# Window attention and a gated MLP on one core: the hidden units dealt to partitions in groups of four

## The chip, the cores and the metric

The kernel runs on 1 core of one Trainium2 chip. The metric is device time in microseconds (us) of one execution. Before the change the median of 3 runs is 228.85 us (227.75 to 229.1).

## The reference

Sliding-window attention with four sink positions, then an MLP whose activation has a learned slope for each hidden unit. Inputs and output are float32; the kernel computes in bf16 with float32 sums.

```python
B, H, S, D = 4, 8, 768, 64            # n_sink = 4, window = 128
scores = scale * np.matmul(q, k.transpose(0, 1, 3, 2))
keep = is_sink | in_window            # pos < 4, or 0 <= i - j < 128
scores = np.where(keep, scores, -1000000000.0)
a = softmax(scores)
x = np.matmul(a, v)                   # as (3072 tokens, 512)
...
h = x @ w_in                          # w_in (512, 2048)
g = h * (1.0 / (1.0 + np.exp(-beta * h)))   # beta (2048,)
out = g @ w_out                       # w_out (2048, 512)
```

## The kernel before

**Tiles and stages.** The 3072 tokens are cut into 8 tiles of 384. An attention *unit* n (of 32) is one pair of heads for one tile: q and k are transposed so that the 64 head elements lie on partitions, scores are taken 128 keys at a time, ACT takes the exponential, DVE multiplies by the mask, PE multiplies with v, DVE normalises. Four units fill `xT` for one tile (512 model elements on 4 x 128 partitions).

The MLP of a tile has 16 *blocks* m of 128 hidden units (`NM` = 16). For one block PE runs four matmuls (c = 0 to 3) of 384 columns into one PSUM bank: the stationary operand is a 128 x 128 piece of `w_in16`, the moving one a piece of `xT` (L814, "hidden matmul"). ACT takes tanh of beta/2 times the result (L822; the scale is a column of `beta_half`, one value for each partition), and DVE makes `g` (L835). The projection (L843) then multiplies `g[:, m, 128 tokens]` (stationary) with `w_out16[:, m, :]` (moving, 512 columns) and sums over the 16 blocks. Which hidden unit lies on which partition of which block is free, as long as w_in's columns, beta and w_out's rows agree.

**Layouts in memory.** Before, block m holds the units 128m to 128m+127, unit 128m+p on partition p. w_in is loaded in 4 pieces of 512 columns by POOL (L578), w_out in 8 pieces of two blocks by POOL (L583), both cast to bf16 by the DMA. In a w_out piece each partition gets two rows of w_out that lie 128 rows apart in memory. beta comes as a 16 x 128 tile by one DMA on ACT's queue (L864), is transposed by PE with a float32 identity (L883) and halved by DVE (L885).

**Order of the work.** Operations are declared in program order, with what they read and write. A planner (`Prog`) then places them: for each engine it takes the operation that can start first, with durations written into the code and an estimate of when each DMA lands. What comes out is one fixed order per engine, with semaphore waits in it. Changed transfers therefore change the order on all engines, and each engine works strictly in that order.

**Queues.** SP issues the float32 loads of q and k for units 0 to 11 (L522). POOL casts them to bf16 (L621; at the start DVE casts q), and issues the loads of w_in, w_out, v (L542), and, for units 12 and up, the landing DMAs of q, k (L552) and v (L561), which SP then turns with DMA transposes (L567). POOL does its casts and its DMA issues in one order.

Some loads are gated on others by `after`, so that they do not crowd the DMA engines: unit n of 8 to 11 waits for the w_out piece that holds block 2n-12, and two v loads wait for the pieces of blocks 6 and 8 (L969 to L978). The units 4 to 7 wait for w_in's second piece.

Of the kernel before, what the change touches and what calls it, by code (L numbers as in the profile page):

```python
# [5 lines left out]
F32 = mybir.dt.float32  # L6
AF = mybir.ActivationFunctionType
ALU = mybir.AluOpType

B, H, S, D = 4, 8, 768, 64  # L10
NSINK, WINDOW = 4, 128
DM, DF, NOUT = 512, 2048, 512
NTOK = B * S
NPAIR = B * (H // 2)
SCALE = 1.0 / (D ** 0.5)
# [3 lines left out]
TT = 384  # L19
NT = NTOK // TT  # L20
NU = 4 * NT
NM = DF // 128
# [33 lines left out]
AGENDA = {}  # L56
for n in range(4, 8):
    for step, at in (("in", n - 4), ("sink", 16), ("a", 16), ("b", 16), ("av", 17), ("out", 18)):
        AGENDA.setdefault(at if step == "in" else at + 1 * (n - 4), []).append((n, step))
for n in range(8, NU):  # L60
    for at, step in STEPS.items():
        AGENDA.setdefault(FIRST[n] + at, []).append((n, step))
# [294 lines left out]
def bass_streamingllm_window__then__act_swish_beta_kernel(  # L357
# [21 lines left out]
    def sb(name, shape, dtype):  # L379
        ctx.append(nc.sbuf_tensor(name, list(shape), dtype))  # L380
        return ctx[-1].__enter__()
# [5 lines left out]
    xT = sb("xT", (128, 4, NTOK), BF16)  # L387
    w_in16 = sb("w_in16", (128, 4, DF), BF16)
    w_out16 = sb("w_out16", (128, NM, NOUT), BF16)
    beta_stage = sb("beta_stage", (16, 128), F32)  # L390
    beta_half = sb("beta_half", (128, NM), F32)
    ones = sb("ones", (128, 128), BF16)
    zeros = sb("zeros", (128, 384), BF16)
    ident = sb("ident", (128, 128), BF16)
    ones32 = sb("ones32", (32, 32), F32)
    ident32 = sb("ident32", (32, 32), F32)
    scratch = sb("scratch", (32, 1), F32)
    mask = [sb(f"mask{z}", (128, 6, 128), BF16) for z in range(2)]
    add_mask = sb("add_mask", (128, 6, 128), BF16)
# [25 lines left out]
    op = P.op  # L425

    def pe(n):
        return {"busy": 2.5 + n / 2.4, "lag": 260.0}
# [4 lines left out]
    def dve(t):  # L433
        return {"busy": t, "lag": 140.0}
# [4 lines left out]
    def select(out_ap, in_ap, patt, cmp, fill, base, cm, r, w, after=()):  # L439
        op("gp", lambda e: e.affine_select(out_ap, in_ap, patt, cmp, fill, base=base,  # L440
                                           channel_multiplier=cm), r=r, w=w, busy=290.0, lag=100.0, after=after)
# [75 lines left out]
    def load_qk(n, x, after=(), queue="sp"):  # L517
        _, _, half, pb = place(n)
        name = "qk"[x]
        s = rows_of((q, k)[x], n, 1, half, 3)  # L520
        d = stage[name][pb][:, :, 3 * half:3 * half + 3, :].rearrange("p h c d -> p h (c d)")
        op(queue, lambda e: e.dma_start(d, s), w=[(name + "_stage", pb, half)], after=after,  # L522
           dma=f"{name}{pb}_{half}", seq="loads " + queue, **transfer(2 * TT * D * 4, 290 if n not in (1, 2) or x else 170, 520.0))

    def load_v32(x, c):

        src = v[0, 4 * x:4 * x + 4, c * 128:c * 128 + 128, :].rearrange("h p d -> p h d")
        op("act", lambda e: e.dma_start(v_stage[:, c, 4 * x:4 * x + 4, :], src), w=[("v_stage", x, c)],
           dma=f"v{x}{c}", seq="loads act", **transfer(4 * 128 * D * 4, 240, 520.0, 0.45))
# [41 lines left out]
           w=[("qkT", pb, half)], dma=f"t{pb}{half}", busy=1300.0, lag=1300.0)  # L571

    w_in_src = moe_w_in.rearrange("(c p) f -> p c f", p=128)
    w_out_src = moe_w_out.rearrange("(m p) n -> p m n", p=128)

    def load_w_in(m, ms, after=()):
        here = slice(m * 128, (m + ms) * 128)
# [2 lines left out]
           dma=f"wi{m}", late=0.0 if m else 800.0, **transfer(DM * ms * 128 * 4, 385, 740.0, 3.0))  # L580

    def load_w_out(m, ms, after=()):
        op("gp", lambda e: e.dma_start(w_out16[:, m:m + ms, :], w_out_src[:, m:m + ms, :]), after=after,  # L583
           w=[("w_out", mm) for mm in range(m, m + ms)],
           dma=f"wo{m}", **transfer(ms * 128 * NOUT * 4, 416, 740.0, 3.0))

# [224 lines left out]
    def hidden_matmul(i, c):  # L811
        T, m = i // NM, i % NM
        bank, name = hidden_bank(i)
        op("pe", lambda e: e.matmul(  # L814
            bank, w_in16[:, c, m * 128:(m + 1) * 128], xT[:, c, T * TT:(T + 1) * TT],
            start=(c == 0), stop=(c == 3)),
           r=[("w_in", c, m), ("xT", T, c)], w=[name], **pe(TT))

# [22 lines left out]
    def project(T, t, m, bank, name, eng="act", cols=slice(0, NOUT), queue="sp"):  # L841
# [19 lines left out]


    constants()
    op("act", lambda e: e.dma_start(beta_stage[:, :], moe_beta.rearrange("(m p) -> m p", p=128)),  # L864
       w=["beta_stage"], dma="beta", busy=500.0, lag=100.0)
    for n in range(4):
        for x in range(2):
            load_qk(n, x)
    for c in range(6):
        load_v32(c // 3, c % 3)  # L870
    op("act", lambda e: e.activation(scratch[:, :], ones32[:, 0:1], AF.Exp, bias=0.0, scale=1.0),
       r=["ones32"], w=["scratch"], busy=1500.0)
    cast(0)
# [4 lines left out]
    cast(2)  # L878
    load_sinks(1, [("v", 1, 0, 0)])

    select(ident32[:, :], ones32[:, :], [[1, 32]], ALU.is_equal, 0.0, 0, -1, ["ones32"], ["ident32"])
    transpose_first(0)
    op("pe", lambda e: nc.tensor.transpose(acc[1][:, 0:16], beta_stage[:, :], ident32[0:16, 0:16]),  # L883
       r=["beta_stage", "ident32"], w=["acc1"], **pe(64))
    op("dve", lambda e: e.tensor_scalar(beta_half[:, :], acc[1][:, 0:16], 0.5, None, ALU.mult),  # L885
       x=["acc1"], w=["beta"], **dve(100.0))

    def first_scores(n):
        pairs = [("s0", "s1"), ("h0", "h1")] if n < 3 else [("s0", "s1"), ("tr", "av")]
# [48 lines left out]
    for s in range(-2, S_END + NM):  # L938
# [27 lines left out]
        if s in casts:  # L966
            cast(casts[s])
        if s == 0:
            for m in range(2, 8, 2):  # L969
                load_w_out(m, 2, [("w_in", 0, 0)])  # L970
        if s == 2:
            for m in range(8, NM, 2):
                load_w_out(m, 2, [("w_in", 0, 8)])
            for n in range(8, 12):
                for x in range(2):
                    load_qk(n, x, [("w_out", 2 * n - 12)])
            for c in range(2):
                load_v(2, c, [("w_out", 2 * c + 6)])  # L978
        if s == 23:
            load_v(2, 2)  # L980
        if s in lands:
# [59 lines left out]
```

## Time and profile before

| what | value |
|---|---|
| median of 3 runs | 228.85 us (227.75 to 229.1) |
| the profiled execution | 228.59 us, its span 226.9 us |
| granted TensorE clock | 1.0 throughout |
| PE busy | 220.0 us (97% of the span), 1761 matmuls |
| ACT, DVE, POOL busy | 141.3, 132.6, 125.7 us |
| DMA packets | 96901, 28.92 MB |

The span is what lies between the first and the last instruction; 1.7 us of the execution are outside it. The costliest groups and the transfers that matter here:

```profile
L822 ACT ACTIVATE th<-h_ps,beta_half 128x384 f32<-128x384 f32 x120 | 69.4, 581 | 59.7 <-PE h_ps L814 59.1
L843 PE MATMUL acc<-w_out,g 128*128 128x512 bf16 x368 | 99.7, 380 | 0.0
L814 PE MATMUL h_ps<-xT,w_in 128*128 128x384 bf16 x480 | 96.2, 326 | 0.0
...
q_stage<-in_q_dram SPq DMA_DIRECT2D x12, 192.0 KB, 7.4
k_stage<-in_k_dram SPq DMA_DIRECT2D x12, 192.0 KB, 7.9
w_in<-in_moe_w_in_dram POOLq DMA_DIRECT2D x4, 512.0 KB, 6.8
w_out<-in_moe_w_out_dram POOLq DMA_DIRECT2D x8, 256.0 KB, 9.6
```

A group's line gives the source line, the engine, what it writes and reads, its shape and count, then its busy us, the mean ns of one, and the idle time before it with its releaser. The mean of a matmul (326 ns) is longer than the distance between two, since matmuls overlap in the array. A DMA line gives the KB that one issue writes and the median us from issue to landing. "PEld" is the load of stationary weights, "SPq" and "POOLq" are issues by these engines' queues.

### The profile page before, as it was taken

The page shows a single profiled execution, that of the slowest core. Times are in us where ns is not written, and L with a number is a line of the kernel's source. Part 1 is how long each engine was busy: PE and PEld are TensorE (multiplying, and loading weights), DVE is VectorE, ACT ScalarE, POOL GpSimd, SP SyncE. Part 2 cuts the span into 40 slices and gives each one's busy share as a digit, 9 for nine tenths or more (in the row PEclk, how much of TensorE's full clock was granted, in tenths as well). Part 3 has the DMA queues.
Part 4 walks back from the last instruction along what each step waited for, and adds up shares of the span by engine and source line. Part 5 has one row for each costly group of instructions (what it writes and reads, how often), then busy time and mean ns, then how long its engine had stood idle before and what let it go on. Part 6 is the DMA issues. An engine that isn't in the chain of part 4 may idle for free.

```text
span 226.9 us, 4463 instructions
## 1 busy us (share of the span) xinstructions
PE 220.0 (97%) x1761; PEld 122.1 (54%) x1761; DVE 132.6 (58%) x264; ACT 141.3 (62%) x224; POOL 125.7 (55%) x191
## 2 busy tenths in 40 slices
PE   7999989999999999999999999999999999999995
PEld 4665545555555555555555555555555555555454
DVE  5466777488975776566565656555656564443200
ACT  1877796197586877566657766666656755555311
POOL 4689992899994979695939396876300000000000
PEclk9999999999999999999999999999999999999999
DMA  6999999999998999999999999998921012110122
GB/s 172 251 172 179 276 194 205 257 228 139 118 138 124 124 117 151 120 167 144 116 113 135 99 138 147 96 165 119 94 80 53 20 57 64 49 46 0 58 83 92
DMA packets 96901, 28.92 MB, mean 127 GB/s; under 512 B 83424, under 2 KB 93936, under 8 KB 96880
## 3 DMA queue, kind: packets, MB, share of 16 engines
q0 software_dynamic: 59232, 10.92, 65.7%
q1 hardware_dynamic: 34304, 16.79, 34.3%
q10 hardware_dynamic: 3344, 0.93, 1.9%
q8 instruction: 14, 0.23, 0.5%
q14 instruction: 7, 0.06, 0.1%
HBM read 27.34 MB, written 6.29 MB: 148 GB/s over the span
## 4 chain that ended last, share of the span: by engine, by line
PE 73%; DMA 15%; POOL 8%; issue 2%; SPq 1%; ACT 0%; POOLq 0%; ACTq 0%
PE acc L843 32%; PE h_ps L814 29%; DMA k_stage<-in_k_dram 8%; DMA w_out<-in_moe_w_out_dram 4%; PE s_ps L727 4%; PE s_ps L770 4%; POOL qk L621 3%; DMA w_in<-in_moe_w_in_dram 2%; POOL land L552 2%; PE h_ps L843 2%; POOL v_aug L561 1%; PE s_ps L759 1%; PE s_ps L670 1%; SPq L522 1%; POOL v_aug L532 0%
## 5 line engine op out<-in xcount | busy, mean ns | idle before, releaser
L822 ACT ACTIVATE th<-h_ps,beta_half 128x384 f32<-128x384 f32 x120 | 69.4, 581 | 59.7 <-PE h_ps L814 59.1
L843 PE MATMUL acc<-w_out,g 128*128 128x512 bf16 x368 | 99.7, 380 | 0.0
L814 PE MATMUL h_ps<-xT,w_in 128*128 128x384 bf16 x480 | 96.2, 326 | 0.0
L835 DVE SCALAR_TENSOR_TENSOR g<-th,h_ps 128x384 bf16<-128x384 f32 x120 | 65.6, 550 | 44.8 <-ACT th L822 44.0
L814 PEld LDWEIGHTS h_ps<-xT,w_in 128*128 128x128 bf16 x480 | 45.6, 98 | 39.8 <-issue 0.8
L843 PEld LDWEIGHTS acc<-w_out,g 128*128 128x128 bf16 x368 | 32.8, 98 | 28.8 <-issue 3.6
L552 POOL DMA_DIRECT2D land<-in_q_dram x40 | 30.2, 760 | 24.0 <-DVE rden L779 24.0
L552 POOL DMA_DIRECT2D land<-in_k_dram x40 | 30.3, 761 | 0.0
L561 POOL DMA_DIRECT2D v_aug<-in_v_dram x40 | 30.2, 760 | 0.0
L735 ACT ACTIVATE E<-s_ps 128x1536 bf16<-128x1536 f32 x20 | 28.8, 1442 | 0.0
L741 DVE TENSOR_TENSOR E<-E,mask 128x1536 bf16<-128x1536 bf16 x20 | 19.2, 958 | 16.4 <-ACT E L735 16.4
L851 ACT ACTIVATE out_sb<-acc 128x512 f32<-128x512 f32 x23 | 13.7, 596 | 7.6 <-PE acc L843 7.4
L770 PEld LDWEIGHTS s_ps<-v_aug,E 128*128 128x128 bf16 x336 | 15.2, 97 | 3.2 <-issue 1.2
L770 PE MATMUL s_ps<-v_aug,E 128*128 128x65 bf16 x336 | 16.8, 193 | 0.0
L707 ACT ACTIVATE E<-s_ps 128x768 bf16<-128x768 f32 x17 | 13.7, 811 | 4.3 <-PE s_ps L700 4.2
L781 DVE TENSOR_TENSOR o_norm<-s_ps,rden 128x384 bf16<-128x384 f32 x28 | 15.6, 556 | 0.8
L714 DVE TENSOR_TENSOR E<-E,mask 128x768 bf16<-128x768 bf16 x16 | 9.0, 572 | 2.0 <-ACT E L707 1.3
L727 PE MATMUL s_ps<-qkT 64*128 64x256 bf16 (+2 forms) x144 | 10.1, 254 | 0.0
L759 PE MATMUL s_ps<-v_sink,E_sink 128*128 128x130 bf16 x48 | 9.3, 219 | 0.0
L621 POOL CAST qk<-k_stage 128x384 bf16<-128x384 f32 x12 | 6.5, 544 | 4.7 <-DMA k_stage<-in_k_dram 4.4
L673 ACT ACTIVATE E_sink<-s_ps 128x384 bf16<-128x384 f32 x16 | 7.8, 490 | 1.5 <-PE s_ps L670 1.5
L727 PEld LDWEIGHTS s_ps<-qkT 64*128 64x128 bf16 x144 | 4.9, 94 | 7.1 <-issue 5.8
(75 smaller groups left out, 155.2 us busy)
## 6 DMA issues: line engine op xcount, KB each, us to landing
out_dram<-out_sb SPq DMA_DIRECT2D x23, 256.0 KB, 2.7
q_stage<-in_q_dram SPq DMA_DIRECT2D x12, 192.0 KB, 7.4
k_stage<-in_k_dram SPq DMA_DIRECT2D x12, 192.0 KB, 7.9
w_in<-in_moe_w_in_dram POOLq DMA_DIRECT2D x4, 512.0 KB, 6.8
w_out<-in_moe_w_out_dram POOLq DMA_DIRECT2D x8, 256.0 KB, 9.6
land<-in_q_dram POOLq DMA_DIRECT2D x40, 48.0 KB, 3.7
land<-in_k_dram POOLq DMA_DIRECT2D x40, 48.0 KB, 4.0
v_aug<-in_v_dram POOLq DMA_DIRECT2D x40, 48.0 KB, 3.4
```

What stands on the lines that cost most here:

```text
L552: op("gp", lambda e, d=d, s=s: e.dma_start(d, s), w=[("land", pb, half, x, hh)], after=after, dma=f"l{pb}{half}{x}{hh}", **transfer(TT * D ...
L561: op("gp", lambda e, d=d, s=s: e.dma_start(d, s), w=[("v", pb, 3 * half + c, hh) for c in range(3)], after=after, dma=f"lv{pb}{half}{hh}", ...
L707: op("act", lambda e: e.activation(both, src[:, :, 0:TT], AF.Exp, bias=0.0, scale=SCALE), x=list(names), w=[("E", n % NE, c)], **act(768))
L727: op("pe", lambda e, at=at, w=w, kb=kb, qb=qb, nq=nq, hh=hh, rows=rows, bank=bank: e.matmul(s_ps[:, 2 * hh + bank, at:at + w], keys_of(pb, ...
L735: op("act", lambda e: e.activation(E[z][:, :, :], src, AF.Exp, bias=0.0, scale=SCALE), x=list(S_NAMES), w=[("E", z, 0), ("E", z, 1)], **ac ...
L741: op("dve", lambda e: e.tensor_tensor(E[z][:, :, :], E[z][:, :, :], m.unsqueeze(1).to_broadcast([128, 2, 768]), ALU.mult), r=[("E", z, 0), ...
L770: last=(x == len(kbs) - 1): e.matmul(av_ps[:, at + hh * D1:at + hh * D1 + D1], E[z][:, hh, col:col + 128], v_aug[:, pb, hh, kb, 0:D1], sta ...
L781: op("dve", lambda e: e.tensor_tensor(o_norm[o][:, :, :, :].rearrange("p m h d -> p (m h) d"), src[:, :, 0:D], rden[z][:, :].unsqueeze(2). ...
L814: op("pe", lambda e: e.matmul(bank, w_in16[:, c, m * 128:(m + 1) * 128], xT[:, c, T * TT:(T + 1) * TT], start=(c == 0), stop=(c == 3)), r= ...
L822: op("act", lambda e: e.activation(th[i % 3][:, :], bank, AF.Tanh, bias=0.0, scale=beta_half[:, m:m + 1]), x=[name], r=["beta"], w=[("th", ...
L835: op("dve", lambda e: e.scalar_tensor_tensor(g[T % 2][:, m, :], th[i % 3][:, :], 1.0, bank, ALU.add, ALU.mult), r=[("th", i % 3)], x=[name ...
L843: op("pe", lambda e: e.matmul(bank[:, 0:width], g[T % 2][:, m, t * 128:(t + 1) * 128], w_out16[:, m, cols], start=(m == 0), stop=(m == NM ...
```

## The change

Hidden unit 512g + 4p + j now lies on partition p of block 4g + j (`PER` = 4). So on one partition the four rows of w_out of a group g are neighbours in memory, 8 KB in a row. Three layouts follow.

- w_out is loaded in 5 pieces of 2, 2, 4, 4, 4 blocks; in each piece a partition reads one run of 4 or 8 KB instead of two runs of 2 KB.
- w_in is loaded as before. The stationary operand of a hidden matmul is now every fourth column of a group of 512.
- beta is read by DMA straight into (128, 16): 4 runs of 16 bytes on each partition. The DMA is issued on ACT's queue behind the six first loads of v instead of ahead of them. The float32 identity, the PE transpose and PSUM bank use for it are gone; DVE halves beta from SBUF.

The gates of units 8 to 11 move to the pieces of blocks 0, 4, 8 and 12, those of the two v loads to blocks 8 and 12.

```diff
+PER = 4
...
-    beta_stage = sb("beta_stage", (16, 128), F32)
+    beta_raw = sb("beta_raw", (128, NM), F32)
...
-    ident32 = sb("ident32", (32, 32), F32)
...
-    w_out_src = moe_w_out.rearrange("(m p) n -> p m n", p=128)
+    w_out_src = moe_w_out.rearrange("(g p j) n -> p g j n", p=128, j=PER)
...
     def load_w_out(m, ms, after=()):
-        op("gp", lambda e: e.dma_start(w_out16[:, m:m + ms, :], w_out_src[:, m:m + ms, :]), after=after,
+        op("gp", lambda e: e.dma_start(w_out16[:, m:m + ms, :].rearrange("p j n -> p (j n)"),
+                                         w_out_src[:, m // PER, m % PER:m % PER + ms, :].rearrange("p j n -> p (j n)")), after=after,
...
-            bank, w_in16[:, c, m * 128:(m + 1) * 128], xT[:, c, T * TT:(T + 1) * TT],
+            bank, w_in16[:, c, m // PER * 512 + m % PER:m // PER * 512 + 512:PER], xT[:, c, T * TT:(T + 1) * TT],
...
-    op("act", lambda e: e.dma_start(beta_stage[:, :], moe_beta.rearrange("(m p) -> m p", p=128)),
-       w=["beta_stage"], dma="beta", busy=500.0, lag=100.0)
...
+    op("act", lambda e: e.dma_start(beta_raw[:, :].rearrange("p (g j) -> p g j", j=PER),
+                                   moe_beta.rearrange("(g p j) -> p g j", p=128, j=PER)),
+       w=["beta_raw"], dma="beta", busy=500.0, lag=300.0)
+    op("dve", lambda e: e.tensor_scalar(beta_half[:, :], beta_raw[:, :], 0.5, None, ALU.mult),
+       r=["beta_raw"], w=["beta"], **dve(100.0))
...
-    select(ident32[:, :], ones32[:, :], [[1, 32]], ALU.is_equal, 0.0, 0, -1, ["ones32"], ["ident32"])
...
-    op("pe", lambda e: nc.tensor.transpose(acc[1][:, 0:16], beta_stage[:, :], ident32[0:16, 0:16]),
-       r=["beta_stage", "ident32"], w=["acc1"], **pe(64))
-    op("dve", lambda e: e.tensor_scalar(beta_half[:, :], acc[1][:, 0:16], 0.5, None, ALU.mult),
-       x=["acc1"], w=["beta"], **dve(100.0))
...
         if s == 0:
-            for m in range(2, 8, 2):
-                load_w_out(m, 2, [("w_in", 0, 0)])
+            load_w_out(2, 2, [("w_in", 0, 0)])
+            load_w_out(4, 4, [("w_in", 0, 0)])
         if s == 2:
-            for m in range(8, NM, 2):
-                load_w_out(m, 2, [("w_in", 0, 8)])
+            for m in range(8, NM, 4):
+                load_w_out(m, 4, [("w_in", 0, 8)])
             for n in range(8, 12):
                 for x in range(2):
-                    load_qk(n, x, [("w_out", 2 * n - 12)])
+                    load_qk(n, x, [("w_out", 4 * (n - 8))])
             for c in range(2):
-                load_v(2, c, [("w_out", 2 * c + 6)])
+                load_v(2, c, [("w_out", 4 * c + 8)])
```

The planner's new order differs from the old one mostly where the transfers do. On POOL: the stretch from the first w_out issue to the casts of units 8 to 11 reads as follows (casts are "unit, operand"; `land` is a landing DMA of L552, `v` a load of L542, `lv` one of L561).

```
before: w_out 0, 4q, 4k, w_out 2, 5q, w_out 4, 5k, w_out 6, 6q, 6k, w_out 8, 7q, 7k, w_out 10, 12, 14,
        v, land q, v, land q, land k, land k, 8q, 8k, v, 9q, 9k, land q x2, 10q, 10k, land k x2, lv x2, ..., 11q, ..., 11k
after:  w_out 0, 4q, 4k, w_out 2, 5q, 5k, w_out 4, 6q, w_out 8, 6k, 7q, w_out 12, 7k,
        8q, land q x2, land k, v, land k, 8k, v x2, 9q, 9k, land q x2, land k x2, lv, 10q, 10k, lv, 11q, 11k
```

On PE, the two score matmuls of unit 7 that stood ahead of the first projections now stand behind the first eight of them, and the transposes of units 8 to 10 are split into a group for q and one for k with other work between them; the rest moves by a few matmuls. On DVE the halving of beta moves from the start to a place behind the second `o_norm`.

## The prediction

> **What bounds the kernel now.** I read the busy time by stages first, because the page's 97% for PE is a mean over a start, a mixed stage and a long steady one. The stretches end where the PE timeline changes: the first hidden matmul (17.3 us), the first projection (35), the last wait of any size (60).
>
> ```profile
> 0.00:17.30 17.30, 15.48 (x177) 10.08 (x178) 9.85 (x28) 10.09 (x16) 11.22 (x27) 1.00 0.98 198
> 17.30:35.00 17.70, 15.98 (x132) 8.90 (x130) 13.39 (x25) 14.73 (x27) 16.98 (x34) 1.00 1.35 216
> 35.00:60.00 25.00, 24.34 (x226) 13.71 (x223) 18.66 (x40) 15.27 (x25) 19.95 (x29) 1.00 1.53 193
> 60.00:211.00 151.00, 151.00 (x1158) 82.01 (x1157) 89.18 (x170) 98.33 (x152) 77.58 (x103) 1.00 1.00 105
> ```
>
> The columns are stretch, length, then busy us and count of PE, PEld, DVE, ACT, POOL, the granted clock, the DMA share and GB/s. From 60 us on PE never idles at full clock: nothing there can get shorter unless PE has less to do, and only an added PE cost makes it longer. The idle that a change of loads can move lies before: 17.70-15.98 = 1.7 us and 25.00-24.34 = 0.7 us. Whatever PE waits longer before 60 us goes to the end undiminished.
>
> Second, the PE timeline around those waits:
>
> ```profile
> 26.78 0.34 PE L634 MATMUL s_ps<-ident,qk 128*128 128x128 bf16 x3 [0.29 <-POOL qk L621]
> 34.81 0.34 PE L700 MATMUL h_ps<-qkT 64*128 64x128 bf16 x4 [0.36 <-ACT E L707]
> 35.08 1.04 PE L843 MATMUL acc<-w_out,g 128*128 128x512 bf16 x4
> 45.98 0.33 PE L634 MATMUL s_ps<-ident,qk 128*128 128x128 bf16 x3
> 50.56 0.34 PE L634 MATMUL s_ps<-ident,qk 128*128 128x128 bf16 x3 [0.18 <-POOL qk L621]
> 59.16 0.34 PE L634 MATMUL s_ps<-ident,qk 128*128 128x128 bf16 x3 [0.47 <-POOL qk L621]
> ```
>
> L634 transposes q and k of one unit after POOL has cast them. Three of these waits are for POOL. So, third, POOL and SP at the units 8 to 11, which the change regates:
>
> ```profile
> 32.37 2.11 POOL L583 DMA_DIRECT2D w_out<-in_moe_w_out_dram  x3
> 38.97 0.89 POOL L542 DMA_DIRECT2D v_aug<-in_v_dram  x1 [4.48 <-DMA w_out<-in_moe_w_out_dram]
> 40.49 0.74 POOL L552 DMA_DIRECT2D land<-in_q_dram  x1 [0.64 <-DVE rden L779]
> 44.38 0.52 POOL L621 CAST qk<-q_stage 128x384 bf16<-128x384 f32 x1
> 45.31 0.51 POOL L621 CAST qk<-k_stage 128x384 bf16<-128x384 f32 x1 [0.42 <-DMA k_stage<-in_k_dram]
> ...
> 37.41 0.37 SPq L522 DMA_DIRECT2D q_stage<-in_q_dram  x1
> ```
>
> (The last line is SP's.) Unit 8's q is issued at 37.41, when the piece of w_out it is gated on lands; by its landing event it is there at 43.82 (6.4 us), k at 45.26. POOL has put four issues in front of the casts, and the casts come just as the data do. PE needs k's cast at 45.98: no slack.
>
> Last, the cost of a weight load:
>
> ```profile
> L814 PEld LDWEIGHTS h_ps<-xT,w_in x480: 95/98/99, 17.6 to 211.4; 128*128 128x128 bf16 x160
> L770 PEld LDWEIGHTS s_ps<-v_aug,E 128*128 128x128 bf16 x336 | 15.2, 97 | 3.2 <-issue 1.2
> L770 PE MATMUL s_ps<-v_aug,E 128*128 128x65 bf16 x336 | 16.8, 193 | 0.0
> ```
>
> **The change, part by part.** The sum is made on the profiled execution: 228.59 us, of which the span is 226.9 and 1.7 lie around it; the median of the three runs, 228.85, is 0.1% above.
>
> Strided weights (L814). 512 hidden matmuls read their stationary operand at a step of four bf16, 8 bytes. No row shows a strided weight load. In the PE timeline eight hidden matmuls start over 1.30 us (20.61 to 21.91): 162 ns each, and that is the cover. L770's twelve matmuls of 65 columns start over 0.38 us (10.29 to 10.67), 32 ns apart, each with a 97 ns load of its own: loads overlap, and a packed one costs the stream no more than 32 ns. A strided one may thus take five times a packed one's share, or 64 ns longer by its whole duration, before a matmul waits. I take 0. The far end: duration doubled and nothing overlapped, (196-162) ns x 512 = 17 us. Below zero is excluded, since the load is hidden already. The Trainium skill (SBUF — State Buffer, the note on cachelines under "Door 1") says accesses run at full rate with two hits on each 16-byte line, and up to a step of eight bf16; at 8 bytes there are just two. No run shows it; by it this term is 0 as well.
>
> Start. Gone are POOL's select of ident32 (0.29 us; POOL waits 2.0 us for k at 4.97 anyway), PE's 0.28 us beta transpose (filler matmuls surround it), and nothing for ACT: seven issues remain seven. DVE's read of beta moves from 4.06 to behind o_norm of the second unit, about 14 us; queued behind it is a reciprocal that waits for PE until 15.24, and the first reader of beta is the tanh at 18.65. Beta would have to land after 15 us to hurt; the last v load, next before it on ACT's queue, lands at 11.56. v now goes 0.46 us earlier and meets the first q and k. Bounds: -0.09 (DVE's 0.18 us instruction no longer precedes q's cast at 4.15) and +0.46. I take +0.1.
>
> Beta's transfer. Instead of 16 packets it is 512 of 16 bytes, 32 per DMA engine. The packet records give 9 to 18 ns for 4 bytes and 20 for 256, so 0.3 to 0.6 us of a busy DMA. At 25.0 us PE waits 0.28 us for the last piece of w_in, the end of a backlog; that may grow by 0 to 0.6. I take +0.2.
>
> w_out's transfer. Today 16 packets of 1 KB per engine and piece at 98 ns (their mean is 103); undisturbed pieces land 1.28 us apart. Now 640 row chunks stand for 2048. Plain packets (18 ns at 256 bytes, 84 at 2048) have some 9 ns that size does not explain; applied here, 1.2 us per two rows, and by the copy rate of the 4 KB read, 1.05. PE meets the first piece at 35.08, 0.2 us after it lands at 34.88: -0.1 (bounds 0 and -0.2). Four-row pieces arrive as a whole: rows 4 to 7 at about 38.6, 8 to 11 at 41.2, 12 to 15 by 44; PE wants them, by its new order, at 39.1, 41.9 and 44.8. So 0, with up to +0.6 kept for the last.
>
> POOL around 30 us. Three issues of 0.70 us fall away, but before 38.97 POOL idles 4.48 us: no gain. Two issues now stand ahead of k's casts of units 6 and 7, which end near 31.4 and 33.1 instead of 30.7 and 32.4, and PE follows by 0.65. At 34.18 it then skips the wait for ACT (0.43 with its switch), because the score matmuls behind it are moved past the first projections. Net +0.2. The new PE order has 84 changes between 64 and 128 rows instead of 82, 95 ns each in the timeline: +0.2.
>
> Units 8 to 11. SP's loads of unit 8 are gated on the first piece instead of the third: issued at about 34.9 instead of 37.4. In POOL's new order the cast of q stands ahead of the landing DMAs: q's cast (0.55), two landings for q, one for k (2.25), a v load (0.9), a landing (0.75), then k's cast (0.5): it ends 4.95 us after q lands. With the 6.4 us of before, q lands at 41.3 and k's cast ends at 46.25; with unit 4's 7.3 us (issued 17.96, landed 25.23), at 47.1. PE, by the same durations (24 projections of 216 ns, three attends of 0.53, four transposes out of 0.17, a hidden block of 0.65, scores and switches 1.3), reaches k's transposes 9.6 us after the first projection: 44.6. Stall 1.65 to 2.5, less some 0.3 that PE is late by; I take +1.8. Bounds: 0.25 if q lands before the lands' own gate (40.4), 4.3 if q waits out the w_out backlog and lands at 44. Unit 10 then comes 4.75 us behind unit 9 on POOL, where PE gives it 3.85; its margin takes most of that. Against this, the old waits at 50.56 and 59.16, 0.25 and 0.54 with what precedes them, sit where PE is now late: -0.8 (bounds 0 and -0.8).
>
> Sum: 0 + 0.1 + 0.2 - 0.1 + 0.2 + 0.2 + 1.8 - 0.8 = +1.6 us: 230.2.
>
> **The rivals.** *The loads take turns, no stall at k.* q needs 16 packets of 42 ns per engine, 0.67 us; if engines alternate between queues, q lands about 39 and the term falls to 0.25: 228.6. For it: under competition (41.24 to 45.07) w_out's pieces come 1.9 us apart, so loads do get a third. Against: from 37.41 to 41.24 the pieces still came at 1.28, so q got nothing for 4 us, and unit 4's q landed only with the last of w_in. The Trainium skill (DMA: Bandwidth & Descriptors, "Queues, rings and completion order") has each engine round-robin between rings by packet; by that rule this rival holds, and the two landings speak against it.
>
> *The backlog goes first, harder.* Longer chunks hold an engine longer per turn; q lands at 44, k's cast ends at 49: +4.3+0.5 instead of 1.8: 233.5. The point is q landing after 43.
>
> *Strided loads are exposed.* If a load takes over 162 ns of the stream, 17 us: near 247. For it only that no row shows one.
>
> *The waits dissolve.* If everything PE loses from 17 to 60 us beyond its switches went, 2.4 us: 226.2. It needs ACT's and DVE's waits at 30 to 32 to go too, which the change doesn't touch.
>
> That the change does not do what it says is excluded by the instruction order: five w_out issues of 1024 and 2048 elements per partition.
>
> **How the numbers follow.** Forecast 0.43, turns 0.24, backlog 0.17, strided 0.09, dissolved 0.07. Predicted is the forecast's 230.2, its own range 228.9 to 231.5. The range runs from 227.2, between turns and dissolved, to 233.4, most of the backlog case; strided loads and the tails are left out. One per cent, about what this measurement can tell, is 2.3 us: 226.6 to 231.1. Faster 0.08; same 0.56 (0.33 of the forecast, 0.23 of turns); slower 0.36.
>
> **What would show it.** Hidden matmuls still 162 ns apart and PE without idle after 66 us: the stride is free. PE waiting for POOL's cast before the second group of L634 near 45 us, 1 to 3 us: the forecast; less than 0.4: turns; more than 4: backlog. Unit 8's q landing 6.4 us after its issue decides between them. It is wrong if the start shifts by over 0.5 us, or if PE waits for w_out itself.

## The result, and the profile after

The changed kernel takes 235.29 us (median of 4 runs, 234.79 to 236.03) where the kernel before takes 228.97 us (4 runs, 227.75 to 229.26): a ratio of 1.027 with a 95% interval of 1.024 to 1.031. It is slower by 6.3 us, and it lies 1.9 us above the upper end of the predicted range. The profiled execution took 235.18 us, its span is 233.4 us, and its mean granted clock is 0.993.

Busy time by stages of the changed kernel, first; the columns are those shown for the kernel before:

```profile
0.00:17.30 17.30, 14.23 (x126) 8.59 (x126) 8.49 (x23) 8.16 (x13) 10.44 (x26) 1.00 0.94 191
17.30:35.00 17.70, 16.36 (x157) 11.27 (x156) 14.07 (x26) 14.06 (x27) 14.67 (x31) 1.00 1.36 214
35.00:60.00 25.00, 21.86 (x190) 11.43 (x188) 14.75 (x31) 13.17 (x22) 14.85 (x22) 0.93 1.16 172
60.00:217.00 157.00, 157.00 (x1220) 92.12 (x1219) 95.20 (x184) 102.84 (x160) 82.48 (x110) 1.00 0.95 104
```

From 60 us on PE has no idle time, as before. The loss lies ahead of it: 3.1 us of idle between 35 and 60 us (0.7 before), and there the granted clock is 0.93, so the busy time is partly at half speed. The start is also later: the first hidden matmul comes at 20.76 us (17.32 before), the first projection at 36.99 us (35.08 before). PE ran more of the start at half speed. The record of the clock begins, with full speed, at 12.60 us in this profile and at 6.68 us in that of before, so the 1.00 of the first row says nothing of the time ahead of that. A group of three transposes shows it: 0.34 us at full speed, 0.50 ahead of it. The first line is from the PE timeline of the kernel before, the other two are from that of the changed kernel:

```profile
7.14 0.34 PE L652 MATMUL s_ps<-ident,qk 128*128 128x128 bf16 x3
...
8.53 0.50 PE L654 MATMUL s_ps<-ident,qk 128*128 128x128 bf16 x3
...
12.58 0.34 PE L654 MATMUL s_ps<-ident,qk 128*128 128x128 bf16 x3
```

The PE timeline of the changed kernel around that loss:

```profile
46.60 0.34 PE L636 MATMUL s_ps<-ident,qk 128*128 128x128 bf16 x3
46.77 0.81 PE L816 MATMUL h_ps<-xT,w_in 128*128 128x384 bf16 x4
50.10 0.49 PE L636 MATMUL s_ps<-ident,qk 128*128 128x128 bf16 x3 [2.51 <-POOL qk L623]
50.38 1.06 PE L845 MATMUL acc<-w_out,g 128*128 128x512 bf16 x2
51.24 1.49 PE L816 MATMUL h_ps<-xT,w_in 128*128 128x384 bf16 x4
52.52 0.63 PE L845 MATMUL acc<-w_out,g 128*128 128x512 bf16 x1
```

The first group transposes unit 8's q, the third its k, after 2.51 us of waiting for POOL's cast. What follows is at half clock: four hidden matmuls take from 51.24 to 52.52, 320 ns each, where four take 0.65 us elsewhere. The clock record shows half speed for 3.41 us, from 50.15 to 53.56.

POOL's timeline of the changed kernel says why k's cast is late, with SP's issue of unit 8's q as the last line:

```profile
45.15 0.51 POOL L623 CAST qk<-q_stage 128x384 bf16<-128x384 f32 x1 [12.93 <-DMA q_stage<-in_q_dram]
45.60 1.51 POOL L553 DMA_DIRECT2D land<-in_q_dram  x2
47.11 0.77 POOL L553 DMA_DIRECT2D land<-in_k_dram  x1
47.86 0.93 POOL L543 DMA_DIRECT2D v_aug<-in_v_dram  x1
48.79 0.74 POOL L553 DMA_DIRECT2D land<-in_k_dram  x1
49.53 0.52 POOL L623 CAST qk<-k_stage 128x384 bf16<-128x384 f32 x1
...
34.84 0.37 SPq L523 DMA_DIRECT2D q_stage<-in_q_dram  x1
```

POOL stands still for 12.93 us until q is there, and only then works off five issues that lie between q's cast and k's. q was issued at 34.84 and landed at 45.10, after 10.26 us. k landed at 45.52 and was then free to be cast, but had to wait 4 us for its place in POOL's order.

### The profile page after: what moved, and what is told of

Read it like the earlier page. It is cut to its first block, busy times and chain, and to the rows that moved or that the text cites. A ratio compares the mean times of both kernels' runs of the same rounds, so it can differ in the third digit from the quotient of the medians.

```text
span 233.4 us, 4463 instructions
## 1 busy us (share of the span) xinstructions
PE 223.2 (96%) x1762; PEld 131.2 (56%) x1762; DVE 134.1 (57%) x264; ACT 141.6 (61%) x224; POOL 122.4 (52%) x187
## 4 chain that ended last, share of the span: by engine, by line
PE 76%; DMA 10%; POOL 9%; issue 2%; DVE 1%; ACT 0%; SPq 0%; POOLq 0%; ACTq 0%
PE acc L845 33%; PE h_ps L816 31%; DMA q_stage<-in_q_dram 4%; DMA w_out<-in_moe_w_out_dram 4%; PE s_ps L772 4%; PE s_ps L729 4%; DMA k_stage<-in_k_dram 2%; POOL v_aug L543 2%; PE h_ps L845 2%; POOL w_in L579 1%; POOL qk L623 1%; POOL land L553 1%; PE s_ps L761 1%; POOL v_aug L533 1%; PE s_ps L672 1%
## 5 line engine op out<-in xcount | busy, mean ns | idle before, releaser
L845 PE MATMUL acc<-w_out,g 128*128 128x512 bf16 x368 | 101.4, 382 | 0.0
L816 PE MATMUL h_ps<-xT,w_in 128*128 128x384 bf16 x480 | 97.5, 328 | 0.1
L816 PEld LDWEIGHTS h_ps<-xT,w_in 128*128 128x128 bf16 x480 | 53.3, 114 | 35.1 <-issue 1.4
L623 POOL CAST qk<-q_stage 128x384 bf16<-128x384 f32 x8 | 4.5, 565 | 13.2 <-DMA q_stage<-in_q_dram 13.2
L643 DVE COPY qkT<-s_ps 128x768 bf16<-128x768 bf16 x6 | 5.7, 954 | 5.3 <-PE s_ps L636 5.3
```

What stands on the lines that cost most here:

```text
L816: op("pe", lambda e: e.matmul(bank, w_in16[:, c, m // PER * 512 + m % PER:m // PER * 512 + 512:PER], xT[:, c, T * TT:(T + 1) * TT], start= ...
L845: op("pe", lambda e: e.matmul(bank[:, 0:width], g[T % 2][:, m, t * 128:(t + 1) * 128], w_out16[:, m, cols], start=(m == 0), stop=(m == NM ...
```

## The experiments

Times are medians. The kernel before ran on the same chip each time, and the ratio is to it.

### The parts alone, on the kernel before

**The stride.** Only the stationary operand of the hidden matmuls is read at a step of four; the hidden units then no longer fit beta and w_out's rows.

```diff
-            bank, w_in16[:, c, m * 128:(m + 1) * 128], xT[:, c, T * TT:(T + 1) * TT],
+            bank, w_in16[:, c, m // 4 * 512 + m % 4:m // 4 * 512 + 512:4], xT[:, c, T * TT:(T + 1) * TT],
```

> The kernel before, with one edit: the hidden matmuls read w_in's weights at a step of four columns; w_out and beta stay as they were, so the hidden units of w_in no longer match those of beta and w_out, while every instruction and its order stay. Theory (the stride is hidden behind the 162 ns of a hidden matmul): 228.4 to 229.5 us, hidden matmuls still 162 ns apart, weight loads 114 ns instead of 98 as in the changed kernel. Rival (the stride carries part of the 6.3 us): 230 us or more, PE with gaps between hidden matmuls.

229.09 us, ratio 1.002 [0.9991, 1.0048]. By line, the weight loads of the kernel with the stride alone (minimum, median and maximum duration in ns):

```profile
L814 PEld LDWEIGHTS h_ps<-xT,w_in x480: 111/113/135, 19.8 to 212.2; 128*128 128x128 bf16 x160
```

The load is 15 ns longer than the 98 of before, and still shorter than the 162 ns between two hidden matmuls: it stays hidden. This profile, whose start has the old code, also has its first hidden matmul at 19.42 us, not 17.32: the profiled execution of the kernel before had an early start, and 2 us of the difference between two profiles in the first 20 us need no cause in the code. The clock goes with it: here, too, its record begins late, at 12.16 us.

**beta's path.** The DMA behind the v loads, straight into (128, 16), and DVE's halving from SBUF, as in the change; the transpose and its identity gone.

> The kernel before with the new beta path alone (512 runs of 16 bytes behind the v loads, halved on DVE from SBUF; beta's values then stand at other units than w_in's, the work is the same). Theory (ACT's issue takes over 1 us): table load at 5.9 to 6.5, first hidden matmul at 19.5 to 21, and since waits between 25 and 60 us take some of it up, 0.8 to 2.2 us at the end: 229.5 to 231. Rival (all of the late start is taken up): 228.5 to 229.2.

230.01 us against 229.35, ratio 1.002 [0.9994, 1.0047]. Here and in the changed kernel the same things happen. First ACT, then DVE and POOL of the changed kernel:

```profile
4.75 1.40 ACTq L871 DMA_DIRECT2D beta_raw<-in_moe_beta_dram  x1
6.18 1.28 ACT L876 ACT_TABLE_LOAD   x1 [6.18 <-issue]
...
16.81 2.08 DVE L874 TENSOR_SCALAR beta_half<-beta_raw 128x16 f32<-128x16 f32 x1
18.05 0.84 DVE L781 RECIPROCAL rden<-acc 128x6 f32<-128x6 f32 x1
...
17.04 1.82 POOL L445 MEMSET k_sink<- 128x2048 bf16 x1
```

ACT's issue of beta takes 1.40 us (0.43 before), and the table load behind it starts at 6.18 instead of 4.68; the six v issues ahead of it also took longer, 3.92 us instead of 3.37. DVE's halving takes 2.08 us instead of 0.18: it ends when POOL's memset ends. All of it together is 0.2% of the time, which is not clear of nothing, and by the interval at most 0.5%.

**The rows of w_out.** Two-row pieces of 2 KB runs, nothing else; rows and hidden units then don't match.

```diff
-    w_out_src = moe_w_out.rearrange("(m p) n -> p m n", p=128)
+    w_out_src = moe_w_out.rearrange("(g p j) n -> p g j n", p=128, j=4)
```

> The kernel before, with only the rows of w_out dealt as in the change: eight pieces of two rows, each a run of 2048 bytes for a partition, order of all engines unchanged; w_in's columns and beta stay as before, so rows and hidden units do not match and the output is another. Theory (longer chunks do not make the load faster, and cost only where a gated load takes turns with them; here unit 8's q, gated late at 37.4, gets 16 x (173+42) ns = 3.4 us at worst beside the backlog): 228.5 to 229.6, ratio 0.998 to 1.003. w_out's last piece lands 44 to 45. Rival (longer chunks hold up q and k whatever the gate): q lands after 45 instead of 43.8, PE waits 1 us or more at the casts: 230 to 232.

228.95 us, ratio 0.9997 [0.9973, 1.002]. Its last piece lands at 44.76 us (45.07 before, 44.90 changed): longer runs don't speed the load up. Unit 8's q, issued at 37.59, landed at 44.59 and cost nothing, because this order leaves q and k next to each other on POOL.

**The gates.** Units 8 to 11 and the two v loads wait for the pieces of the changed kernel; w_out keeps its 1 KB chunks and eight pieces.

```diff
-                    load_qk(n, x, [("w_out", 2 * n - 12)])
+                    load_qk(n, x, [("w_out", 4 * (n - 8))])
-                load_v(2, c, [("w_out", 2 * c + 6)])
+                load_v(2, c, [("w_out", 4 * c + 8)])
```

> The kernel before with the gates of the changed one alone: units 8 to 11 wait for the pieces of w_out with blocks 0, 4, 8, 12, the two v loads for blocks 8 and 12; pieces of two blocks, layout, weights and beta as before. POOL's order again has unit 8's q cast ahead of the landing DMAs and its k cast behind them. Theory (order and backlog, not the long rows): q of unit 8 lands within 1 us of the last pieces of w_out (43 to 45), PE waits 2.5 us or more for k's cast and runs at half clock after it: 231.5 to 233.5 us. Rival (the wait needs the long rows, which hold the DMA engines): q lands at about 41.5, wait under 1.5 us, 229 to 230.2.

228.84 us, ratio 0.9995 [0.9964, 1.0027]: no loss. This was against my theory of then, that the earlier issue and POOL's new order were enough. POOL's timeline of this kernel:

```profile
40.42 0.50 POOL L621 CAST qk<-q_stage 128x384 bf16<-128x384 f32 x1 [6.21 <-DMA q_stage<-in_q_dram]
...
45.98 0.52 POOL L621 CAST qk<-k_stage 128x384 bf16<-128x384 f32 x1
```

The order is the changed kernel's in the main: two casts with six issues between them. But q, issued at 34.17, landed at 40.36, after 6.19 us and not 10.26. What was missing was something that makes q late.

### Parts taken back, on the changed kernel

**Unit 8's gate one piece later.** The planner then puts the issues of `land` and v ahead of unit 8's casts.

```diff
-                    load_qk(n, x, [("w_out", 4 * (n - 8))])
+                    load_qk(n, x, [("w_out", (4, 4, 8, 12)[n - 8])])
```

> The changed kernel with one number changed: unit 8's loads wait for w_out's piece of block 4 instead of block 0. The planner then puts the landing DMAs ahead of unit 8's casts on POOL, as before the change. Theory (PE's 2.5 us wait near 47 is POOL's order: k's cast stands five DMA issues behind q's, and q is late): the wait falls under 0.6 us, the half clock after it (3.4 us) is gone, and with it 2.5 + 1.6 = about 4 us: 230.7 to 232. Rival (unit 8's data come too late in any order, because loads wait out the w_out backlog): a wait of 2 us or more stays, 234 to 235.5.

230.56 us, ratio 1.0073 [1.004, 1.0105], 0.1 us below the expected range: 4.7 us come back. That fits a loss that hangs on unit 8's load and casts, but it moves the gate and the order together.

**An earlier start.** Once beta's DMA is the first on ACT's queue; once the planner is told that its issue takes 1.5 us, so that it places six more filler matmuls.

```diff
-       w=["beta_raw"], dma="beta", busy=500.0, lag=300.0)
+       w=["beta_raw"], dma="beta", busy=1500.0, lag=300.0)
```

> The changed kernel with beta's DMA (and its halving) declared ahead of the v loads, so that ACT issues it first. Theory (as the seventh issue on ACT it takes 1.40 us and holds up ACT's table load, the first copy of q, PE, and through PE's idle time the clock): issue near 0.5 us, table load at about 4.7 instead of 6.2, clock full before 8 instead of 12.6, first hidden matmul at 17.3 to 18.0 instead of 20.8, and 1.5 to 2.5 us less in all: 232.8 to 233.8. Rival (512 runs of 16 bytes cost 1.4 us to issue wherever they stand): table load still at about 6.1 and 235 us.

> The changed kernel with the planner told that beta's issue takes ACT 1.5 us instead of 0.5: nothing moves but filler matmuls, of which PE gets six more ahead of the first scores and some later. Theory (the clock stays at half until 12.6 us because PE idles 1.43 us at 6.7): full clock from about 7 us, first hidden matmul at 19.3 to 19.8 instead of 20.8, of which up to 1 us reaches the end: 234.0 to 235.0. Rival (the clock comes late for another reason): full clock only after 11 us and 235.3.

234.49 us (1.0251 [1.0219, 1.0282]) and 234.46 us (1.0263 [1.0206, 1.0321]): 0.8 us less each by the medians, but both intervals overlap that of the changed kernel, so it is not shown that either gains.

The first one missed what I expected of it. With beta in front its issue took 0.48 us, but then the six v issues took 4.63 us, the table load still came at 5.99 and the first hidden matmul at 20.05. The kernel with long chunks and beta's old path (shown below) has 4.55 us for the same six issues, its padded twin in the same order 3.38. So they vary by over 1 us whatever beta does, and it isn't shown that beta's issue is what makes the table load late.

The second one's time is in its range. Its first projection comes at 35.88 us, 1.1 us earlier than in the changed kernel, but PE's wait for unit 8's k, from its timeline, is longer:

```profile
49.44 0.29 PE L636 MATMUL s_ps<-ident,qk 128*128 128x128 bf16 x1 [3.19 <-POOL qk L623]
```

Of the 1.1 us that the start gains, the longer wait takes 0.7: k's cast hangs on the load, not on PE.

**beta by other ways, with the later gate.** Loaded as 4 x 512 and transposed by PE; or issued by SP and halved by ACT.

```diff
-    op("act", lambda e: e.dma_start(beta_raw[:, :].rearrange("p (g j) -> p g j", j=PER),
+    op("sp", lambda e: e.dma_start(beta_raw[:, :].rearrange("p (g j) -> p g j", j=PER),
...
-    op("dve", lambda e: e.tensor_scalar(beta_half[:, :], beta_raw[:, :], 0.5, None, ALU.mult),
+    op("act", lambda e: e.activation(beta_half[:, :], beta_raw[:, :], AF.Copy, bias=0.0, scale=0.5),
```

> The changed kernel with unit 8's gate at block 4 and beta loaded as 4 rows of 512 ahead of v and transposed by PE (four small transposes with a step of four columns), so that it stands at the dealt units; w_out's long rows and the strided weights stay. Theory (gate and beta path are the whole loss, the layout itself costs or gains under 0.3%): 228.2 to 229.6. Rival (pieces of four rows or the stride cost something of their own): 230 or more.

> The changed kernel with unit 8's gate at block 4, beta's 16-byte runs issued by SP behind its first eight loads, and the halving on ACT. Theory (what costs is ACT's time for the issue): table load at 4.2 to 4.8, 228.2 to 229.6. Rival (the 16-byte runs slow the DMA engines for all loads, whoever issues them): first hidden matmul later than 19 and 230 or more.

230.74 us (1.0079 [1.0039, 1.0118]) and 229.72 us (1.0018 [0.9988, 1.0048]). The first misses its range by over 1 us, so the later gate and another path for beta do not give back the whole loss; the second is 0.1 us above its range. It is the best form of the change that was found, level with the kernel before, and no version beat that.

### What makes q late

The packet records of the DMA engines show it. Counted here are, from the issue of unit 8's q on, the first of its 256 packets of 768 bytes (16 on each of 16 engines), its landing, and how many packets of q or k and how many chunks of w_out all engines start in one us while both are there. The chunk's time is the mean of its records.

```
kernel             chunk of w_out   issued  first   q, w_out per us  landed  issue to landing
gates alone        1 KB,  96 ns     34.17   37.75   127, 129         40.36    6.19
two-row pieces     2 KB, 172 ns     34.15   37.69    86,  77         41.31    7.16
changed kernel     4 KB, 322 ns     34.84   38.34    54,  43         45.10   10.26
```

Two things are to be seen. From issue to first packet it is 3.5 to 3.6 us whatever the chunk (1.1 us for the first load of the kernel, when the engines are idle). What fills these 3.5 us no run shows. From then on about one packet of q is started for one chunk of w_out. The records don't name the engine, but the starts of q's packets repeat most often after 0.12 to 0.14, 0.18 to 0.20 and 0.34 to 0.36 us in the three kernels, a little under the time of one chunk and one packet, as they would if each engine took one of each in turn. So q needs 16 turns, each as long as one chunk and one packet (47 to 49 ns in this company): 16 x (96+48) = 2.3 us, 16 x (172+48) = 3.5 us, 16 x (322+47) = 5.9 us. From first packet to landing it took 2.6, 3.6 and 6.8 us; the 0.1 to 0.9 us above the estimate are not explained. By this reading the chunk sets the landing.

That is still a reading of records from kernels that differ in more than the chunk. So the next kernel keeps everything but the chunk.

**The changed kernel with padded rows.** Each row of the bf16 copy of w_out is followed by 32 unused elements, which cuts what the DMA engines write into 1 KB again. The order on all five engines is that of the changed kernel, instruction by instruction.

```diff
-    w_out16 = sb("w_out16", (128, NM, NOUT), BF16)
+    w_out16 = sb("w_out16", (128, NM, NOUT + 32), BF16)
...
-        op("gp", lambda e: e.dma_start(w_out16[:, m:m + ms, :].rearrange("p j n -> p (j n)"),
-                                         w_out_src[:, m // PER, m % PER:m % PER + ms, :].rearrange("p j n -> p (j n)")), after=after,
+        op("gp", lambda e: e.dma_start(w_out16[:, m:m + ms, 0:NOUT],
+                                         w_out_src[:, m // PER, m % PER:m % PER + ms, :]), after=after,
```

> The changed kernel, with every row of the bf16 copy of w_out followed by 32 unused elements. The order on all engines is that of the changed kernel, instruction by instruction; only the chunks that the DMA engines write become 512 elements (1 KB) again instead of 1024 and 2048. Theory (in a turn-taking DMA engine unit 8's q needs 16 turns, and each waits for one chunk of w_out: 16 x (325+42) ns = 5.9 us with 4 KB chunks, 16 x (98+42) = 2.2 us with 1 KB): q issued about 34.9 lands near 41 instead of 45.1, as in the kernel that has the gates alone (40.36), POOL's cast of k ends near 46, PE waits under 1 us there, and keeps its clock: 231 to 232.3, 3 to 4 us below the changed kernel. Rival A (the order of POOL and the backlog as such make q late, whatever the chunk): q lands at 45, stall 2.5 us, half clock, 235. Rival B (the start alone makes the wait, since it comes 1.7 us late): same as A.

230.50 us (9 runs, 229.87 to 231.1), ratio 1.0069 [1.0047, 1.0092]: 4.8 us below the changed kernel, more than the 3 to 4 expected. q was issued at 35.45 and landed at 41.73, after 6.28 us. POOL's two casts and PE's timeline of the padded kernel:

```profile
41.78 0.63 POOL L623 CAST qk<-q_stage 128x384 bf16<-128x384 f32 x1 [8.49 <-DMA q_stage<-in_q_dram]
...
46.38 0.52 POOL L623 CAST qk<-k_stage 128x384 bf16<-128x384 f32 x1
```

```profile
46.68 0.34 PE L636 MATMUL s_ps<-ident,qk 128*128 128x128 bf16 x3
46.85 0.81 PE L816 MATMUL h_ps<-xT,w_in 128*128 128x384 bf16 x4
47.51 0.33 PE L636 MATMUL s_ps<-ident,qk 128*128 128x128 bf16 x3
47.89 0.38 PE L845 MATMUL acc<-w_out,g 128*128 128x512 bf16 x1
...
50.21 0.33 PE L636 MATMUL s_ps<-ident,qk 128*128 128x128 bf16 x3
```

PE gets to unit 8's q within 0.1 us of the changed kernel (46.68, 46.60) and to its k without a wait: at 47.51 instead of 50.10, 2.6 us. At unit 9's q it is 50.21 against 54.40, 4.2 us, the other 1.6 being the half clock. The spans of the two profiles differ by 4.2 us. Order and start are the same in both (the first hidden matmul at 20.84 and 20.76 us), so the two rivals that needed only these have fallen. The price is paid elsewhere, and doesn't matter: w_out's last piece lands at 47.03 instead of 44.90, as it would if it gave way more often.

**Two-row pieces.** Eight pieces of 2 KB chunks, the changed gates.

```diff
-            for m in range(8, NM, 4):
-                load_w_out(m, 4, [("w_in", 0, 8)])
+            for m in range(8, NM, 2):
+                load_w_out(m, 2, [("w_in", 0, 8)])
```

> The changed kernel with eight pieces of two rows (2048-byte chunks) instead of 2, 2, 4, 4, 4; the gates name the same blocks, POOL again has unit 8's cast of q ahead of the landings, and two landings, a v load, a landing, a v load and a landing between it and the cast of k. Theory (turns): q issued near 36.2 needs 16 x (173+42) ns = 3.4 us of turns behind what is queued, lands near 41.5 to 42.5; k's cast ends near 47.5; PE waits 0.5 to 1.5 us: 231 to 233.5. Rival (order alone): as the changed kernel, 235. Rival (chunks alone, the order costs nothing): 229 to 230.

230.79 us, ratio 1.0075 [1.0049, 1.01], 0.2 us below the expected range. q, issued at 34.15, landed at 41.31, between the ends, and PE had no wait for k at all. The expected wait of 0.5 to 1.5 us did not come: PE got to unit 8's k at 47.55 us, when POOL's cast of it (46.98 to 47.50) was just over.

**The planner told that loads land late.** The weight of a w_out load in the planner's estimate is 30 instead of 3; gates and chunks stay.

```diff
-           dma=f"wo{m}", **transfer(ms * 128 * NOUT * 4, 416, 740.0, 3.0))
+           dma=f"wo{m}", **transfer(ms * 128 * NOUT * 4, 416, 740.0, 30.0))
```

> The changed kernel; only the planner's weight for a load of w_out is 30 instead of 3, so that its model lets q and k of units 8 to 11 land later. Gates and transfers stay; on POOL the landings and two v loads of that stretch move ahead of unit 8's casts, and PE, DVE and ACT are reordered by some places. Theory: unit 8's q still lands near 45, but POOL has nothing between q's and k's cast, so k's cast ends 1.1 us after q lands, near 46.2 instead of 49.9; PE waits under 1 us and the clock does not drop: 230.5 to 232. Rival (what costs is the late landing, not the order): PE still waits 2 us or more near 46 to 50 and 234 to 235.

230.59 us, ratio 1.0066 [1.0043, 1.009]. q landed only at 43.59, 9.37 us after its issue, but the issues of `land` and v now stand ahead of the casts, which follow each other. POOL's timeline of this kernel:

```profile
46.49 0.90 POOL L543 DMA_DIRECT2D v_aug<-in_v_dram  x1
47.38 0.52 POOL L623 CAST qk<-q_stage 128x384 bf16<-128x384 f32 x1
47.83 0.51 POOL L623 CAST qk<-k_stage 128x384 bf16<-128x384 f32 x1
```

k's cast ended at 48.34 and not near 46.2, but PE, whose order moved with it, takes q and k together at 48.32 and doesn't wait; the time is in the expected range. So it needs both to lose the 4 to 5 us: a q that is late, and an order that counts on it being early. Either one taken away gives them back.

### What is left

The padded kernel is still 0.7% (1.7 us) above the kernel before. The last two kernels have beta's old path (its values then are dealt otherwise than the hidden units), once with the padding and once without; their orders are the same.

> The changed kernel with the padded rows (1 KB chunks) and with beta's old path: first on ACT's queue as a 16 x 128 tile, transposed by PE, halved by DVE at the start. beta's values then do not match the dealing of the hidden units. What remains of the change: the strided weights, five pieces, the new gates and POOL's and PE's new order. Theory (of the 1.7 us that the padded kernel is above before, the start through beta's path is some 1.2: it was 1.3 between the two kernels with the later gate): 228.8 to 229.6, ratio 1.000 to 1.004. Rival (pieces, gates and order cost it, not the start): 230 to 230.8, ratio 1.005 to 1.009.

> The same kernel without the padding: 2 and 4 KB chunks, beta's old path, the order of all engines the same as in the other kernel of this call. Theory (w_out's pieces, and so the issue of unit 8's q, move with the start by a part only; q lands 9 to 10 us after its issue; PE gets there earlier and waits longer, loses its clock): 233.5 to 234.7, that is 4 to 5.5 us above its padded twin, as 4.8 separates the two with the new path. Rival (the late start is needed for the wait, and with the early one it is gone): under 231.

231.74 us (6 runs, 230.3 to 232.18), ratio 1.0124 [1.0094, 1.0154], and 236.26 us (6 runs, 233.92 to 237.49), ratio 1.0333 [1.029, 1.0376]. The chunk is worth 4.5 us here as well, so the wait doesn't need the late start; the PE timeline of the second one has it, from an earlier place:

```profile
45.48 0.81 PE L817 MATMUL h_ps<-xT,w_in 128*128 128x384 bf16 x4
49.22 0.34 PE L637 MATMUL s_ps<-ident,qk 128*128 128x128 bf16 x3 [2.92 <-POOL qk L624]
```

Both missed their ranges: the first was expected at 228.8 to 229.6 us, the second at 233.5 to 234.7. With beta's old path the time is not lower but 1.2 us higher, although the first hidden matmul comes at 18.12 us instead of 20.84. That doesn't clear beta's path, for the planner makes another order with it on all engines. In the profiles the loss lies in different places:

```
kernel                  first projection   later than before   span longer than before
padded                  37.30              2.2                 2.4
two-row pieces          36.82              1.7                 1.7
planner's weight 30     37.40              2.3                 2.3
padded, old beta path   35.75              0.7                 2.3
```

In the first three, nearly all of the 1.7 to 2.4 us is there when the first projection starts; in the last, most of it comes after. The number of pieces isn't it, since the two-row kernel has eight and stands as high as the padded one with five, and five pieces with the later gate and beta issued by SP are level with before. A late start alone isn't it either: the kernel with the stride alone has its first projection 1.5 us late and loses 0.2%, the one with the gates alone 0.9 us late and loses nothing. So in the first three the rest goes with the start; why their later waits don't take it up, and what the old path loses after the start, stays open.

## Why the prediction was wrong

It gave 230.2 us, +1.6 us on the kernel before, with a range up to 233.4; it was +6.3.

- **The step that failed** is "With the 6.4 us of before, q lands at 41.3 and k's cast ends at 46.25". The 6.4 us were measured in company of 1 KB chunks, and I carried them over to 4 KB ones. In place of 6.4 the runs showed 10.26 us, and 6.28 us with nothing changed but the chunk. The bound I had put on it, q landing at 44, was 1.1 us short.
- **Around that step the mechanism held.** I took 4.95 us from q's landing to the end of k's cast on POOL; it was 45.10 to 50.05. PE waited there and for this cast, 2.51 us where I took +1.8 with an upper bound of 4.3. That the wait came out near my figure is luck: k's cast ended 3.8 us later than in my sum (50.05, not 46.25), and PE came 3.0 us later, at 47.6 instead of 44.6. Of these 3.0, 2 us are the first projection (36.99), and 1 us the way from there to k's transposes: 10.6 us, where I took 9.6 and the terms that I listed add up to 9.4.
- **The missing term** is the clock: after the wait PE ran 3.41 us at half speed, which cost 1.6 us. No part of my sum or of the rivals allowed for a stall to cost more than itself, though the page of before showed a clock of 1.0 in every stage, which a new stall could end.
- **The rivals.** "The loads take turns" had the rule that the packet records show, and I priced it wrongly: 16 x 42 ns for q's own packets, without the chunk that each turn waits for and without the 3.5 us to the first packet. Those 3.5 us were also my evidence against it ("q got nothing for 4 us"): they are the same at every chunk size, so they don't tell of chunks that went first. The Trainium skill (DMA: Bandwidth & Descriptors, "Queues, rings and completion order") has each engine go round its queues packet by packet, where a packet is typically some nine to seventeen descriptors. The records agree on the going round, with 127 packets of q to 129 chunks of w_out in one us, but the spacing of q's packets points to a switch after every single one. "The backlog goes first, harder" named the length of a chunk as the cause and a landing at 44. Its sum is wrong by 0.3: 4.8 in place of 1.8 gives 233.2, not 233.5. With the half clock that is 234.8 us, near the measured 235.3, but by luck: it has PE wait 4.8 us for k, where 2.51 were measured, and it has nothing for the 1.7 us that stay open.
- **The start**, +0.1 with bounds to +0.46, was mis-sized as I described it: the first hidden matmul moved by 3.4 us between the two profiles, and a shift of over 0.5 us was my own sign of being wrong. Some 2 us of it also come without the change (19.42 in the kernel with the stride alone). I had counted ACT's seven issues as seven, and not that one of them with 512 runs takes 1.40 us, nor that DVE's halving may wait, nor that PE's clock may come later. As time beta's path alone was little: 0.2% [-0.06%, +0.47%]; what its DMA gains at the front is not clear of noise. Beta's transfer (+0.2) is in that.
- **Right terms.** The stride at 0 (ratio 1.002, its interval holds 1; a load of 113 ns under a spacing of 162 ns). w_out's load no faster (-0.1): last landing 44.90 against 45.07, first 34.82 against 34.88. The waits of before at 50.56 and 59.16 (-0.8) are gone: PE has no wait for POOL after 50.10.
- **Not told apart**: +0.4 for POOL around 30 us and the switches. It may lie in the open 1.7 us.

## What to carry to other kernels

The time that a gated load takes to land is not a property of that load: where it takes turns with another queue, it grows with its number of packets times the other one's chunk, so a change that only makes chunks longer can delay a transfer that it never touches. Look at what an in-order engine has been told to do between two casts of the same unit, because an order made for an early landing pays for a late one with everything in between. And allow for the clock when you price a new stall of 2 to 3 us on PE: here 2.5 us of waiting cost another 1.6 us.

## What the runs showed of the hardware

- A wait of PE of 2.51 us was followed by 3.41 us at half clock, and so were waits of 2.15 us (beta's DMA first) and 3.19 us (the planner told). In these records every stretch between two changes of the clock is a multiple of 3.41 us (37.55 is eleven of them). The Trainium skill (TensorE: Matmul & The Clock Gate, "What's actually happening") gives such a free-running window and has the clock fall after a whole idle one; the length agrees, but here PE had worked from 46.77 to 47.59 and again from 50.10, so the window from 46.74 to 50.15 was not idle throughout. It isn't certain either: the kernel with long chunks and beta's old path kept its clock at 1.0 through a wait of 2.92 us in the execution of 233.92 us, and had 0.978 to 0.993 in its other five, 234.27 to 237.49 us.
- DVE's halving of 128 x 16 float32 in SBUF ended 0.03 to 0.04 us after POOL's memset of `k_sink` in the six profiles where the two overlapped (it was 1.60 to 2.49 us long), and took 0.16 us in one where it was over 0.7 us before the memset began. In five of the six it had begun before the memset, while POOL was issuing a load of w_in. The Trainium skill (SBUF — State Buffer, "Who interferes with whom") says that a DVE instruction in a two-port mode and GpSimd block each other fully for the length of an instruction on a pair of ports that both share. That fits; whether the halving ran in such a mode no run shows.
- 512 packets of 16 bytes took 9 ns each. Their issue took ACT 1.1 to 1.9 us in the kernels that had them behind the v loads, 0.48 us where it came first, and SP 0.47 us.
